# Moving the sums of the Strassen-like forms beside attention, and one rectified tile to VectorE

## The chip, the cores and the metric

The kernel runs on one core of a Trainium2 chip. The metric is device time in microseconds (us) of one execution. The times shown are three runs; a profiled execution gives the trace. Engines are named as the profile names them: PE (TensorE), PEld (its weight loads), DVE (VectorE), ACT (ScalarE), POOL (GpSimd), SP (SyncE, which issues nearly all DMAs).

## What is computed

Attention over 2 batches of 8 heads, 768 tokens and 64 columns a head, with a local window and global keys; its 1536 x 512 result x goes through a mixture of four experts, weighted by given probabilities, and then through a last layer.

```python
scores = scale * q @ k.T + bias          # bias: slope by head times distance; masked outside the window
a = exp(scores - max); a = a / (a.sum(-1) + 1e-09)
x = (a @ v) as (1536, 512)
for e in range(4):
    h = np.maximum(x @ w1[e], 0.0)       # 512 -> 1024
    out += p[:, e:e + 1] * (h @ w2[e])   # 1024 -> 512
h = out @ w_in; solu = h * softmax(h); ln = normalise(solu) * g_ln
result = ln @ w_out
```

All float32. Matmuls run on a pair of float32r parts: each operand is cast ("high") and the remainder ("low") is kept beside it, so each product is three matmuls (high by high, high by low, low by high).

## The kernel before

Each expert is cut into two half-experts, he = 0 to 7, of 512 hidden columns. The 1536 tokens are blocks of columns of the transposed x, held as `xh` and `xl`. For he = 0, `moe` (L644) goes over four blocks, (0, 256), (256, 256), (512, 512) and (1024, 512). In each block `gemm_groups` (L436) yields four groups `g1` (first product: 12 matmuls by `wR`, L452, then the rectified tile `fhh` on ACT, L458, and its remainder `fhl` on DVE, L459) and four groups `g2` (12 matmuls by `wV`, L471, then the scaling by the probabilities on DVE, L477 for he = 0 and L481 after, where POOL adds the result, L482). The first three blocks run inside attention; the fourth needs the last tokens and runs after it.

For he = 1 to 7 the third block goes as before, and the first 1024 tokens are taken as a pair: `paired_groups` (L498) forms two first products of 512 columns from seven smaller ones, with matrix forms of the Strassen kind. On the weights' side `form_steps` (L324, sums on POOL L337 to L340) makes the forms into `fwS` for each he. On x's side they are made once, by `x_forms` (L558): for j = 0 and 1 eight sums on POOL (`tt`, L575), four casts to high parts on ACT (`high`, L579) and four low parts on DVE (`low`, L582). Three forms go to `xt`; the fourth replaces `xh` and `xl` in columns 512 to 1023, which must no longer be needed raw.

`x_forms` is called when the fourth block of he = 0 begins (L659) and puts its steps into `st.due`; `tick` (L374), called after each group, carries out what is due, among the splits of the next weights (`split_of`: the high part on ACT, L288, the low part on POOL, L296), the weight forms and the loads. The steps of j = 0 and 1 stand five ticks apart, sixteen ticks in all: over the eight groups of he = 0's fourth block and the first seven of he = 1's third. `st.formed`, set by the last, lets the conversion of the last layer's weights start (`conv_steps`, L353, every third tick).

Attention is written out by hand in steps; from t = 14 each step takes two units of one token block and two heads (loop at L1156). In order: `scores` (L862, PE), `soft_pair` (L891), which normalises the probabilities `p` of the units t - 2 and t - 1 (DVE, L898 to L902), runs what is `late` (the low part `xl` of a finished token block, L975) and computes the masked scores (DVE, L915) and their exponentials (ACT, L920) of units t and t + 1; then `pull`, which lets `moe` issue groups up to a share of time; `stage_b` (transposes, L941, copied by ACT, L943); `pull` again; `stage_c` (the product with v, L963, and for a finished token block `xh` on ACT, L974). The last exponentials belong to t = 46; t = 48 and 50 finish. After the loop the last `late` makes the last `xl`, and `rest_of_moe` runs what is left. Every engine works its own queue in the order written here; the program fixes it.

Of the kernel before, what the change touches and what calls it, by code (L numbers as in the profile page):

```python
# [8 lines left out]
F32 = mybir.dt.float32  # L9
# [3 lines left out]
I64 = mybir.dt.int64  # L13
U32 = mybir.dt.uint32
AF = mybir.ActivationFunctionType
ALU = mybir.AluOpType
# [35 lines left out]
def kernel(ctx, tc, ep, qk, vp, nn, pr, wall, w64, gl, out):  # L52
# [158 lines left out]
    def stream(arm):  # L211
# [25 lines left out]
        st.rest = 0  # L237
        st.in_pb = 3 if arm == "f" else 0
        st.pre = None
        st.formed = False  # L240
        if arm == "f":

# [193 lines left out]
        def gemm_groups(he, blk, last, given=None):  # L436


            c0, n = blk
            cols = slice(c0, c0 + n)  # L440
            hh, hl = [None] * 4, [None] * 4

            def g1(ft):
                made = st.pre if he == 0 and c0 == 0 else None
                if made:
                    ps = made[ft]
                else:
                    ps = st.psp.tile([128, 512], F32, tag="g", name=f"{arm}g")
                w = st.pieces[8 * he + ft].rearrange("p w (k f) -> p w k f", k=4)
                for k in range(0 if made else 4):  # L450
                    for i, (a, b) in enumerate(((0, xh), (0, xl), (1, xh))):
                        nc.tensor.matmul(ps[:, :n], lhsT=w[:, a, k], rhs=b[:, k, cols],  # L452
                                         start=(k == 0 and i == 0), stop=(k == 3 and i == 2))
                    if k < 3:
                        yield 3 * n / 2.4
                th = st.hp.tile([128, n], F32R, tag="hh", name=f"{arm}hh")
                tl = st.hp.tile([128, n], F32R, tag="hl", name=f"{arm}hl")
                nc.scalar.activation(th, ps[:, :n], AF.Relu)  # L458
                nc.vector.scalar_tensor_tensor(out=tl, in0=ps[:, :n], scalar=0.0, in1=th.bitcast(F32),  # L459
                                               op0=ALU.max, op1=ALU.subtract)  # L460
                hh[ft], hl[ft] = th, tl
                if last and he == 0:
                    st.free["R", ft] = 1
                yield 3 * n / 2.4

            def g2(dt):
                ps = st.psp.tile([128, 512], F32, tag="g", name=f"{arm}g")
                w = st.pieces[8 * he + 4 + dt].rearrange("p w (k f) -> p w k f", k=4)
                for k in range(4):
                    for i, (a, b) in enumerate(((0, hh), (0, hl), (1, hh))):  # L470
                        nc.tensor.matmul(ps[:, :n], lhsT=w[:, a, k], rhs=b[k],  # L471
                                         start=(k == 0 and i == 0), stop=(k == 3 and i == 2))
                    if k < 3:
                        yield 3 * n / 2.4
                a = acc[:, dt, cols]
                if he == 0:
                    nc.vector.tensor_tensor(out=a, in0=ps[:, :n], in1=pb[:, cols], op=ALU.mult)  # L477
                else:
                    st.tk = getattr(st, "tk", 0) + 1
                    t = tmp2[:, st.tk % 2, :n]  # L480
                    nc.vector.tensor_tensor(out=t, in0=ps[:, :n], in1=pb[:, cols], op=ALU.mult)  # L481
                    nc.gpsimd.tensor_tensor(out=a, in0=a, in1=t, op=ALU.add)  # L482
                    if he == NHE - 1:
                        nc.scalar.copy(xh[:, dt, cols], a)
                        nc.gpsimd.tensor_tensor(out=xl[:, dt, cols], in0=a, in1=xh[:, dt, cols].bitcast(F32),
                                                op=ALU.subtract)
                if last:
                    st.free["V", dt] = he + 1
                    if he == NHE - 1 and dt < 2:
                        st.second.append(14 + dt)  # L490
                yield 3 * n / 2.4

            if given:
                hh, hl = given
                return [g2(i) for i in range(4)]
            return [g1(i) for i in range(4)] + [g2(i) for i in range(4)]
# [61 lines left out]
        def x_forms():  # L558

            g, v = nc.gpsimd, nc.vector  # L560
            hold = {}

            def temps(j):
                if j == 0:
                    hold[j] = [tmp2[:, 0], tmp2[:, 1], krf[:, 2048:2560]]
                else:
                    hold[j] = [st.cvp.tile([128, 256], I64, tag="r64", name=f"{arm}r64", bufs=2).bitcast(F32)
                               for _ in range(2)] + [krf[:, 2048:2560]]

            def steps(j):  # L570
                (b11, b12), (b21, b22) = ([[x[:, k, c0:c0 + HALF].bitcast(F32) for x in (xh, xl)] for c0 in (0, HALF)]
                                          for k in (j, 2 + j))

                def tt(out, in0, in1, op=ALU.subtract):
                    g.tensor_tensor(out=hold[j][out], in0=hold[j][in0] if isinstance(in0, int) else in0,  # L575
                                    in1=hold[j][in1] if isinstance(in1, int) else in1, op=op)

                def high(f, n):
                    nc.scalar.copy(f, hold[j][n])  # L579

                def low(f, h, n):
                    v.tensor_tensor(out=f, in0=hold[j][n], in1=h.bitcast(F32), op=ALU.subtract)  # L582

                def form(f):
                    return xt[:, f, 0, j], xt[:, f, 1, j]

                n4 = [x[:, j, HALF:2 * HALF] for x in (xh, xl)]

                def s0():
                    temps(j)  # L590
                    tt(0, b12[0], b12[1], ALU.add)
                    tt(1, b22[0], b22[1], ALU.add)

                def s1():
                    tt(2, 0, b11[0])
                    tt(2, 2, b11[1])

                def s2():
                    tt(0, 1, 0)

                def s3():
                    high(form(0)[0], 2)
                    tt(1, 1, 2)

                def s4():
                    high(form(2)[0], 0)
                    low(form(0)[1], form(0)[0], 2)

                def s5():
                    high(form(1)[0], 1)  # L610
                    low(form(2)[1], form(2)[0], 0)

                def s6():
                    low(form(1)[1], form(1)[0], 1)
                    tt(0, b21[0], 1)
                    tt(0, 0, b21[1], ALU.add)

                def s8():
                    high(n4[0], 0)

                def s9():
                    low(n4[1], n4[0], 0)
                    if j == 1:
                        st.formed = True

                return [s0, s1, s2, s3, s4, s5, s6, None, s8, s9]

            for j in range(2):
                for i, f in enumerate(steps(j)):
                    if f:  # L630
                        st.due.setdefault(st.now + 1 + 5 * j + i, []).append(f)

        st.x_forms = x_forms
        st.form_steps = form_steps
# [9 lines left out]
    def moe(st, first_blocks):  # L644
# [11 lines left out]
        for j, blk in enumerate(first_blocks):  # L656
            yield blk[0] + blk[1], 0.0
            if j == len(first_blocks) - 1:
                st.x_forms()  # L659
            yield from run(0, blk, j == len(first_blocks) - 1)  # L660
        for he in range(1, NHE):
            yield from run(he, (2 * HALF, 512), False)
# [130 lines left out]
    def fast_arm():  # L793
        st = stream("f")
        with ExitStack() as es:
# [15 lines left out]
            sps = psS.tile([128, 2, 2, 256], F32, name="sps")  # L811
            qs = {s: q_early[s] for s in range(3)}
            vts = {}
            st_p, st_rs, st_pt, st_x = {}, {}, {}, {}
            NU = 4 * NSLOT
            NAT = 2
            N0 = 4 * NAT
# [73 lines left out]
            def soft_pair(t):  # L891

                if t == PAIRS:
                    for _ in stage_n(t - 1):
                        pass
                elif t <= NU:
                    su = st_rs.pop(t - 2)
                    nc.vector.tensor_tensor(out=su, in0=su, in1=eps, op=ALU.add)  # L898
                    nc.vector.reciprocal(out=su, in_=su)
                    for u in (t - 2, t - 1):  # L900
                        p = st_p[u]
                        nc.vector.tensor_tensor(out=p, in0=p, in1=su[:, 2 * (u % 2):2 * (u % 2) + 2].unsqueeze(2)  # L902
                                                .to_broadcast([128, 2, 256]), op=ALU.mult)
                while late:
# [251 lines left out]
            for t in range(PAIRS, NU + 3, 2):  # L1156
# [18 lines left out]
                if t % 4 == 2:  # L1175
                    done = (t - 2) // 4
                    load_v(done + 1)
                if t < NU:
                    for u in (t, t + 1):
                        st.split_piece("act" if u < N0 + 12 and u % 2 else "dve", "pool")  # L1180
                        st.load_piece()
# [179 lines left out]
```

## Time and profile before

| what | value |
|---|---|
| median of 3 runs | 759.12 us (759.12 to 759.14) |
| the profiled execution | 758.87 us, span 757.1 us |
| mean granted clock of PE | 0.993 |
| PE busy | 736.8 us (97% of the span), 3710 matmuls |
| PEld busy | 598.6 us (79%) |
| DVE busy | 445.7 us (59%) |
| POOL busy | 305.1 us (40%) |
| ACT busy | 267.6 us (35%) |
| chain that ended last, by engine | PE 78%, issue 9%, POOL 8%, DVE 3%, ACT 2% |

The span is what the trace covers; the execution's own time has 1.8 us around it. Busy shares are averages over attention (to about 147 us), the half-experts (to about 617 us) and the last layer. PE's records overlap where it streams, so the time of a group is read from start to start.

### The profile page before, as it was taken

How to read it: one execution, taken by the hardware profiler on the slowest of the kernel's cores; microseconds unless marked ns; L12 is line 12 of the kernel's file. 1: busy time of each engine (PE TensorE's matmuls, PEld its weight loads, DVE VectorE, ACT ScalarE, POOL GpSimd, SP SyncE). 2: the span in 40 equal slices, each digit the busy share in tenths (PEclk: the TensorE clock that was granted, in tenths of full speed). 3: DMA queues.
4: the chain of work that ended last, by engine and by line, in shares of the span. 5: the costliest groups of instructions: out<-in, count | busy, mean ns of one | idle time of the engine just before them, and what ended most of it. 6: DMA issues, size and time to landing. Idle time of an engine off the chain costs nothing.

```text
span 757.1 us, 10591 instructions
## 1 busy us (share of the span) xinstructions
PE 736.8 (97%) x3710; PEld 598.6 (79%) x3710; DVE 445.7 (59%) x1026; ACT 267.6 (35%) x601; POOL 305.1 (40%) x294
## 2 busy tenths in 40 slices
PE   8889899998999999999999999999999999999997
PEld 6668777785788888888888888888887888888886
DVE  6777666434376667567577667767622427555541
ACT  5666675333232131231313214113132324233352
POOL 1000010089619708915942960981696271000001
PEclk9999999998999999999999999999999999999999
DMA  8544332011224323324422432441310630222221
GB/s 250 126 133 113 98 84 99 15 42 43 70 84 127 123 84 121 105 74 140 132 84 84 125 112 94 128 126 55 112 29 28 267 150 3 63 74 76 62 74 47
DMA packets 54014, 73.00 MB, mean 96 GB/s; under 512 B 7104, under 2 KB 31936, under 8 KB 53952
## 3 DMA queue, kind: packets, MB, share of 16 engines
q1 hardware_dynamic: 53392, 71.81, 31.3%
q8 instruction: 31, 0.51, 0.3%
q10 hardware_dynamic: 560, 0.43, 0.2%
q14 instruction: 31, 0.25, 0.1%
HBM read 56.46 MB, written 11.56 MB: 90 GB/s over the span
## 4 chain that ended last, share of the span: by engine, by line
PE 78%; issue 9%; POOL 8%; DVE 3%; ACT 2%; DMA 0%; POOLq 0%; ACTq 0%
PE fg L471 29%; PE fg L532 17%; PE fo L771 9%; PE fh L710 9%; PE fg L452 8%; PE sps L862 1%; PE pt L941 1%; POOL scr L482 1%; PE x L963 1%; POOL wV L296 1%; POOL fwS L296 1%; POOL fr L575 1%; POOL tmp L575 1%; ACT p L920 1%; PE wp L136 1%
## 5 line engine op out<-in xcount | busy, mean ns | idle before, releaser
L471 PE MATMUL fg<-fhh,wV 128*128 128x512 f32 (+1 forms) x800 | 248.4, 386 | 4.2 <-ACT fhh L458 3.1
L471 PEld LDWEIGHTS fg<-fhh,wV 128*128 128x128 f32 x800 | 149.9, 189 | 38.2 <-ACT fhh L458 4.4
L482 POOL TENSOR_TENSOR scr<-scr,tmp 128x512 f32<-128x512 f32 x84 | 108.3, 1293 | 165.2 <-DVE tmp L481 165.2
L471 PE MATMUL fg<-fhl,wV 128*128 128x512 f32 (+1 forms) x400 | 153.7, 384 | 1.2 <-DVE fhl L459 1.2
L481 DVE TENSOR_TENSOR tmp<-fg,pb 128x512 f32<-128x512 f32 x84 | 57.9, 689 | 74.5 <-PE fg L471 58.8
L452 PE MATMUL fg<-xh,wR 128*128 128x512 f32 (+1 forms) x320 | 99.5, 383 | 1.4 <-DVE xl L975 1.4
L471 PEld LDWEIGHTS fg<-fhl,wV 128*128 128x128 f32 x400 | 75.7, 189 | 16.7 <-DVE fhl L459 2.5
L452 PEld LDWEIGHTS fg<-xh,wR 128*128 128x128 f32 x320 | 59.5, 188 | 14.9 <-issue 2.0
L459 DVE SCALAR_TENSOR_TENSOR fhl<-fg,fhh 128x512 fp32r<-128x512 f32 (+1 forms) x40 | 26.6, 664 | 69.6 <-ACT fhh L458 69.2
L452 PE MATMUL fg<-xl,wR 128*128 128x512 f32 (+1 forms) x160 | 60.6, 379 | 0.0
L532 PE MATMUL fg<-xt,fwS 128*128 128x512 f32 x252 | 58.4, 390 | 1.0 <-ACT kr L537 1.0
L532 PEld LDWEIGHTS fg<-xt,fwS 128*128 128x128 f32 x252 | 47.2, 188 | 11.2 <-ACT kr L537 1.4
L537 ACT COPY kr<-fg 128x512 f32<-128x512 f32 x42 | 24.3, 584 | 89.4 <-PE fg L532 89.4
L296 POOL TENSOR_TENSOR wR<-fraw,wR 128x512 fp32r<-128x512 f32 x28 | 36.1, 1298 | 48.4 <-ACT wR L288 48.4
L532 PE MATMUL fg<-xh,wR 128*128 128x512 f32 x168 | 55.1, 394 | 0.0
L288 ACT CAST fwS<-kr 128x512 fp32r<-128x512 f32 x28 | 16.0, 619 | 95.0 <-POOL kr L340 95.0
L760 POOL TENSOR_SCALAR fva<-fva 128x1 f32<-128x1 f32 x12 | 3.8, 313 | 109.5 <-ACT scr L759 109.5
L920 ACT ACTIVATE p<-p,mn 128x256 f32<-128x256 f32 x68 | 33.8, 497 | 32.9 <-DVE mn L915 32.9
L771 PE MATMUL fo<-xt,fth 128*128 128x512 f32 (+1 forms) x156 | 45.3, 375 | 0.0
L458 ACT ACTIVATE fhh<-fg 128x512 fp32r<-128x512 f32 (+1 forms) x40 | 23.0, 574 | 54.5 <-PE fg L452 54.5
L519 ACT ACTIVATE fhh<-fg 128x512 fp32r<-128x512 f32 x42 | 24.2, 593 | 44.2 <-DVE fg L541 44.2
L520 DVE SCALAR_TENSOR_TENSOR fhl<-fg,fhh 128x512 fp32r<-128x512 f32 x42 | 28.3, 688 | 18.6 <-ACT fhh L519 18.6
(179 smaller groups left out, 1308.9 us busy)
## 6 DMA issues: line engine op xcount, KB each, us to landing
fraw<-in_wall_dram SPq DMA_DIRECT2D x61, 256.0 KB, 2.7
fr<-in_w_dram SPq DMA_DIRECT2D x32, 256.0 KB, 2.7
w_dram<-fr SPq DMA_DIRECT2D x32, 256.0 KB, 2.5
kr<-in_wall_dram SPq DMA_DIRECT2D x28, 256.0 KB, 2.7
v<-in_vp_dram SPq DMA_DIRECT2D x10, 512.0 KB, 3.6
xt<-w_dram SPq DMA_DIRECT2D x6, 512.0 KB, 10.0
kr<-in_qk_dram SPq DMA_DIRECT2D x22, 128.0 KB, 3.9
out_dram<-scr SPq DMA_DIRECT2D x11, 256.0 KB, 2.2
```

What stands on the lines that cost most here:

```text
L296: e.tensor_tensor(out=w[:, 1], in0=t, in1=w[:, 0].bitcast(F32), op=ALU.subtract)
L452: nc.tensor.matmul(ps[:, :n], lhsT=w[:, a, k], rhs=b[:, k, cols], start=(k == 0 and i == 0), stop=(k == 3 and i == 2))
L459: nc.vector.scalar_tensor_tensor(out=tl, in0=ps[:, :n], scalar=0.0, in1=th.bitcast(F32), op0=ALU.max, op1=ALU.subtract)
L471: nc.tensor.matmul(ps[:, :n], lhsT=w[:, a, k], rhs=b[k], start=(k == 0 and i == 0), stop=(k == 3 and i == 2))
L481: nc.vector.tensor_tensor(out=t, in0=ps[:, :n], in1=pb[:, cols], op=ALU.mult)
L482: nc.gpsimd.tensor_tensor(out=a, in0=a, in1=t, op=ALU.add)
L520: nc.vector.scalar_tensor_tensor(out=tl, in0=src, scalar=0.0, in1=th.bitcast(F32), op0=ALU.max, op1=ALU.subtract)
L532: nc.tensor.matmul(ps, lhsT=w[:, a, j], rhs=x[b][j], start=(i in (1, 2, 5) and j == 0 and m == 0), stop=(j == 1 and m == 2), skip_group_ch ...
L537: nc.scalar.copy(kept[q, i], ps)
L710: nc.tensor.matmul(ps[:, hf], lhsT=a[:, k, cs], rhs=w[:, b], start=(k == 0 and i == 0), stop=(k == 3 and i == 2))
L771: nc.tensor.matmul(ps, lhsT=a[:, fc % 4], rhs=wo[fc][:, b, c0:c0 + n], start=(fc == 0 and i == 0), stop=(fc == 7 and i == 2))
L920: nc.scalar.activation(p[:, a], p[:, a], AF.Exp, bias=mn[:, a:a + 1], scale=-1.0, accum_out=su[:, 2 * (u % 2) + a:2 * (u % 2) + a + 1])
```

## The change

**The sums.** `x_forms` returns eight lists of pieces of work and two last pieces, in place of due times. At attention's step t = 36 the lists are made; from then to t = 50 each step carries out one list at its end: two sums on POOL in each, and casts and low parts one to three steps behind their sums. Up to t = 48 a copy on POOL goes first, of one column of the step's second normalised tile into an unused cell, so that the step's sums start when its normalisations are done. The last two pieces (the fourth forms, which overwrite raw columns) and `st.formed` come where he = 0's fourth block begins. The temporary tiles are now parts of the accumulator that he = 0's fourth block writes later, and `tmp2`.

**The tile.** In he = 0's blocks that run in attention the fourth rectified tile is made on DVE, just ahead of its remainder, in place of ACT.

```diff
-                nc.scalar.activation(th, ps[:, :n], AF.Relu)
+                if ft == 3 and st.wS is None:
+                    nc.vector.tensor_scalar(th, ps[:, :n], 0.0, None, op0=ALU.max)
+                else:
+                    nc.scalar.activation(th, ps[:, :n], AF.Relu)
...
+            temps = [acc[:, j, 1024:1536] for j in range(4)] + [tmp2[:, j] for j in range(2)]
+            def of(j):
+                d12, d1, d2 = temps[3 * j:3 * j + 3]
...
+                add, less = ALU.add, ALU.subtract
+                return [lambda: sums((d12, b12[0], b12[1], add), (d1, d12, b11[0], less)),
+                        lambda: sums((d1, d1, b11[1], less), (d2, b22[0], b22[1], add)),
+                        lambda: sums((d12, d2, d12, less), (d2, d2, d1, less)),
+                        lambda: high(0, d1), lambda: high(2, d12), lambda: high(1, d2),
+                        lambda: low(0, d1), lambda: low(2, d12), lambda: low(1, d2),
+                        lambda: sums((d2, b21[0], d2, less), (d2, d2, b21[1], add)), last]
+            a, b = of(0), of(1)
+            st.unformed += [a[10], b[10]]
+            return [[a[0]], [a[1]], [a[2]], [a[3], b[0]], [a[4], a[6], b[1]], [a[5], a[7], b[2]],
+                    [a[8], b[3], b[4], b[5], a[9]], [b[6], b[7], b[8], b[9]]]
...
-                st.x_forms()
+                for step in (st.x_forms() if st.forms is None else st.forms):
+                    for f in step:
+                        f()
+                for f in st.unformed:
+                    f()
+                st.formed = True
...
                     for u in (t - 2, t - 1):
                         p = st_p[u]
+                        st_last[0] = p[:, 0, 0:1]
...
+                if t == 4 * 8 + 4:
+                    st.forms = st.x_forms()
+                if st.forms:
+                    if t <= NU:
+                        nc.gpsimd.tensor_copy(out=flg[:, 0:1], in_=st_last[0])
+                    for f in st.forms.pop(0):
+                        f()
```

Line numbers of the changed kernel differ a little; in the rows below L298 is L296 of before, L464 L459, L482 L477, L486 and L487 L481 and L482, L889 L915, L871 and L872 L898 and L899, L949 L975, L581 and L586 L582, and L1156 is the copy.

POOL from the end of the weight forms' sums to the scaled sums of he = 1's third block, before (`fr` and `tmp_72` hold the sums of x's forms):

```order
L575 TENSOR_TENSOR kr<-kr,xl 128x512
L296 TENSOR_TENSOR wV<-fraw,wV 128x512
L575 TENSOR_TENSOR fr_1959<-fr_1960,fr_1959 128x512
L296 TENSOR_TENSOR wV<-fraw,wV 128x512
L575 TENSOR_TENSOR fr_1960<-fr_1960,kr 128x512
L296 TENSOR_TENSOR fwS<-kr,fwS 128x512 x2
L296 TENSOR_TENSOR wV<-fraw,wV 128x512
L296 TENSOR_TENSOR fwS<-kr,fwS 128x512
L575 TENSOR_TENSOR fr_1959<-xh,fr_1960 128x512
L575 TENSOR_TENSOR fr_1959<-fr_1959,xl 128x512
L482 TENSOR_TENSOR scr<-scr,tmp_72 128x512
```

and with the change:

```order
L298 TENSOR_TENSOR wR<-fraw,wR 128x512
L298 TENSOR_TENSOR wV<-fraw,wV 128x512 x2
L298 TENSOR_TENSOR fwS<-kr,fwS 128x512 x2
L298 TENSOR_TENSOR wV<-fraw,wV 128x512
L298 TENSOR_TENSOR fwS<-kr,fwS 128x512
L487 TENSOR_TENSOR scr<-scr,tmp_72 128x512
L298 TENSOR_TENSOR wV<-fraw,wV 128x512
```

The sums of x's forms no longer stand between the low parts of the weights.

DVE in the last two steps of attention, before, from the last step's normalisations on:

```order
L902 TENSOR_TENSOR p<-p,su_1693 128x512 x2
L975 TENSOR_TENSOR xl<-x,xh 128x4x128
L477 TENSOR_TENSOR scr<-fg,pb 128x512 x2
L975 TENSOR_TENSOR xl<-x,xh 128x4x128
L459 SCALAR_TENSOR_TENSOR fhl<-fg,fhh 128x512 x4
```

and with the change:

```order
L949 TENSOR_TENSOR xl<-x,xh 128x4x128
L482 TENSOR_TENSOR scr<-fg,pb 128x512
L581 TENSOR_TENSOR xt<-scr,xt 128x512
L482 TENSOR_TENSOR scr<-fg,pb 128x512
L581 TENSOR_TENSOR xt<-tmp_72,xt 128x512
L581 TENSOR_TENSOR xt<-scr,xt 128x512
L581 TENSOR_TENSOR xt<-tmp_72,xt 128x512
L949 TENSOR_TENSOR xl<-x,xh 128x4x128
L586 TENSOR_TENSOR xl<-scr,xh 128x512
L586 TENSOR_TENSOR xl<-tmp_72,xh 128x512
L464 SCALAR_TENSOR_TENSOR fhl<-fg,fhh 128x512 x4
```

Three low parts now stand ahead of the last `xl`, and the two last ones behind it.

DVE at the fourth tile of the block (256, 256), with the change (before, the row L461 is not there, and ACT has one rectifier more):

```order
L889 ISA p,mn<-sps,btab 128x256
L889 ISA mn 128x1
L461 TENSOR_SCALAR fhh<-fg 128x256
L464 SCALAR_TENSOR_TENSOR fhl<-fg,fhh 128x256
L482 TENSOR_TENSOR scr<-fg,pb 128x256
L871 TENSOR_TENSOR su_1123<-su_1123,eps 128x4
L872 RECIPROCAL su_1123<-su_1123 128x4
```

The rectified tile now follows the step's masked scores directly, ahead of the next normalisation. PE's order is the same row by row.

## Rows read from the trace of the kernel before

**Rows 1.** The chain that ended last, in order of time: start us, us, what.

```profile
250.63 10.88 PE fg L471 x48
```

**Rows 2.** PE's timeline: start us, us, engine, line, operation, out<-in, count [idle before <-releaser].

```profile
179.78 0.39 PE L471 MATMUL fg<-fhh,wV 128*128 128x512 f32 x1
...
198.62 0.39 PE L532 MATMUL fg<-xh,wR 128*128 128x512 f32 x1
```

**Rows 3.** Busy time by stretches: PE, PEld, DVE, ACT, POOL; PE clock; DMA.

```profile
130.00:140.00 10.00, 10.00 (x74) 7.59 (x73) 7.21 (x22) 5.92 (x19) 0.00 (x0) 1.00 0.10 30
...
180.00:190.00 10.00, 7.09 (x17) 3.87 (x16) 8.10 (x8) 3.77 (x8) 10.00 (x8) 0.68 0.17 52
```

**Rows 4.** Waits of PE from 100 to 200 us: us in total, times, longest.

```profile
PE fg L471 <- ACT fhh L458: 1.5, 2, 1.0
...
PE fg L471 <- DVE fhl L459: 1.2, 1, 1.2
PE fg L471 <- POOL wV L296: 1.1, 2, 0.9
```

**Rows 5.** POOL's timeline in attention and just behind it.

```profile
103.00 2.54 POOL L575 TENSOR_TENSOR tmp<-xh,xl 128x512 f32<-128x512 f32 x2 [29.20 <-DVE xl L975]
153.97 1.29 POOL L296 TENSOR_TENSOR wR<-fraw,wR 128x512 fp32r<-128x512 f32 x1 [48.43 <-ACT wR L288]
```

**Rows 6.** PE's timeline in attention, at its waits and in two steps.

```profile
45.15 0.63 PE L941 MATMUL pt<-ident,p 128*128 128x128 f32 x4 [2.35 <-DVE p L931]
...
83.39 0.38 PE L471 MATMUL fg<-fhh,wV 128*128 128x256 f32 x1 [1.60 <-ACT fhh L458]
...
84.29 1.64 PE L963 MATMUL x<-pts,v 128*64 128x128 f32 x16
85.85 2.08 PE L862 MATMUL sps<-kr,q 64*128 64x256 f32 x8
...
90.81 1.09 PE L963 MATMUL x<-pts,v 128*64 128x128 f32 x16
91.84 1.13 PE L862 MATMUL sps<-kr,q 64*128 64x256 f32 x8
...
147.01 0.50 PE L452 MATMUL fg<-xh,wR 128*128 128x512 f32 x1 [1.41 <-DVE xl L975]
```

**Rows 7.** Timeline of DVE and POOL, single operations after attention.

```profile
161.55 0.68 DVE L582 TENSOR_TENSOR xt<-kr,xt 128x512 fp32r<-128x512 f32 x1
...
180.54 0.69 DVE L459 SCALAR_TENSOR_TENSOR fhl<-fg,fhh 128x512 fp32r<-128x512 f32 x1 [7.39 <-ACT fhh L458]
180.56 1.29 POOL L575 TENSOR_TENSOR fr<-fr,fr 128x512 f32<-128x512 f32 x1
...
182.32 1.75 DVE L582 TENSOR_TENSOR xt<-kr,xt 128x512 fp32r<-128x512 f32 x1
```

**Rows 8.** Costliest groups: a one-column operation of POOL.

```profile
L760 POOL TENSOR_SCALAR fva<-fva 128x1 f32<-128x1 f32 x12 | 3.8, 313 | 109.5 <-ACT scr L759 109.5
```

**Rows 9.** DVE's timeline in attention, at the fourth tile, beside sums, at the end.

```profile
81.85 0.08 DVE L915 DVE_READ_ACCUMULATOR2_ANT mn<- 128x1 f32 x1
83.37 0.42 DVE L459 SCALAR_TENSOR_TENSOR fhl<-fg,fhh 128x256 fp32r<-128x256 f32 x1 [1.44 <-ACT fhh L458]
...
103.17 0.42 DVE L915 CUSTOM_DVE_ANT_0 p<-sps,btab 128x256 f32<-128x256 f32 x1
...
144.61 0.69 DVE L477 TENSOR_TENSOR scr<-fg,pb 128x512 f32<-128x512 f32 x1 [4.20 <-PE fg L471]
146.26 0.69 DVE L975 TENSOR_TENSOR xl<-x,xh 128x512 fp32r<-128x512 f32 x1 [0.96 <-ACT xh L974]
```

**Rows 10.** ACT's timeline, the last copies of transposed probabilities.

```profile
140.92 1.07 ACT L943 COPY pts<-pt 128x512 f32<-128x512 f32 x2 [2.19 <-PE pt L941]
```

**Rows 11.** Busy time by stretches, at two waits of attention.

```profile
42.00:46.00 4.00, 1.66 (x14) 1.31 (x13) 3.14 (x13) 1.71 (x6) 0.00 (x0) 1.00 0.28 74
...
86.00:88.00 2.00, 2.00 (x9) 1.18 (x9) 0.45 (x2) 0.00 (x0) 0.00 (x0) 0.50 0.00 0
```

More of the change, by code (lines that the diff above doesn't have):

```diff
@@ L239, in stream @@
         st.pre = None
+        st.unformed = []
+        st.forms = None
         st.formed = False
@@ L560, in x_forms @@
             g, v = nc.gpsimd, nc.vector
[L561 to L570, printed above, removed]
+            temps = [acc[:, j, 1024:1536] for j in range(4)] + [tmp2[:, j] for j in range(2)]
@@ L571, in steps @@
+            def of(j):
+                d12, d1, d2 = temps[3 * j:3 * j + 3]
                 (b11, b12), (b21, b22) = ([[x[:, k, c0:c0 + HALF].bitcast(F32) for x in (xh, xl)] for c0 in (0, HALF)]
                                           for k in (j, 2 + j))
-                def tt(out, in0, in1, op=ALU.subtract):
-                    g.tensor_tensor(out=hold[j][out], in0=hold[j][in0] if isinstance(in0, int) else in0,
-                                    in1=hold[j][in1] if isinstance(in1, int) else in1, op=op)
@@ L578, in high @@
[L578 to L631, printed above, removed]
+                def sums(*ops):
+                    for out, in0, in1, op in ops:
+                        g.tensor_tensor(out=out, in0=in0, in1=in1, op=op)
@@ new lines, in high, with low, last @@
+                def high(f, t):
+                    nc.scalar.copy(xt[:, f, 0, j], t)
+                def low(f, t):
+                    v.tensor_tensor(out=xt[:, f, 1, j], in0=t, in1=xt[:, f, 0, j].bitcast(F32), op=ALU.subtract)
+                def last():
+                    h, l = xh[:, j, HALF:2 * HALF], xl[:, j, HALF:2 * HALF]
+                    nc.scalar.copy(h, d2)
+                    v.tensor_tensor(out=l, in0=d2, in1=h.bitcast(F32), op=ALU.subtract)
+                add, less = ALU.add, ALU.subtract
@@ L813, in fast_arm @@
             vts = {}
-            st_p, st_rs, st_pt, st_x = {}, {}, {}, {}
+            st_p, st_rs, st_pt, st_x, st_last = {}, {}, {}, {}, {}
             NU = 4 * NSLOT
```

## The prediction

> **What bounds the kernel now.** I read the clock first (it is granted in full nearly everywhere), then the chain that ended last, the busy time by stretches, the waits of TensorE, and at each wait the timelines of the engines around it. The chain is mostly matmuls: a group of 48 takes 10.88 us [rows 1], so from the end of attention on TensorE is the bound and only its waits can be won. They lie in three places. The first product group of half-expert 1 that multiplies by wV runs from 179.78 to 198.62, 18.84 us for 48 matmuls [rows 2]: 18.84 - 10.88 = 7.96 us lost. In 180 to 190 GpSimd is busy for all of the 10.00 us and TensorE's granted clock averages 0.68 [rows 3]. TensorE's waits there are for the tiles of ScalarE and VectorE (1.5 and 1.2 us) and for GpSimd's wV (1.1 us) [rows 4]; the rest of the 7.96 us is mostly matmuls at the lower clock. Behind all of them stands one queue: GpSimd, idle for 48.43 us up to 153.97 [rows 5], then has the forms' sums, the weights' differences and the weight forms' sums at once, ScalarE's casts wait for those sums, and its rectifiers stand behind the casts. The second place is 83.39 in attention: TensorE had waited 1.60 us for ScalarE's rectified fourth tile [rows 6]. The third is the end of attention, 1.41 us before 147.01 [rows 6].
>
> **The sums of the forms.** Sixteen sums leave the stretch around the first pass: two stood at 103.00 (2.54 us for both), fourteen after 153.97 [rows 5]. At 1.27 us each the fourteen are 17.8 us of GpSimd's time, and with them go six of the eight casts and six of the eight subtractions on the other engines; the last two of each come ahead of the block's first tiles, where TensorE has four products (10.88 us) before it needs any. What is left for GpSimd up to the product group is 4 differences for wR, 8 half-size sums, 4 for wV and 4 for wS. At 1.29 us (a full-size operation) [rows 7] for every one that is at most 20 x 1.29 = 25.8 us, in a stretch of 36 us (153.97 to wV's last use near 190). wV's last two pieces are cast behind the last rectifier; with what then stands ahead on GpSimd (one wV piece, one wS, one scaled sum) the last is ready two short ScalarE operations and four of GpSimd after the first wV tile is due, about 1.0 + 4 x 1.29 = 6.2 us, and is itself due 8.2 us (three tiles of 10.88 / 4) after it. So I take the whole **7.96 us** as won. The later half-experts have this same queue and no waits of TensorE in the views, which is why I do not shave it. Bounds: all of it, or the 1.1 us on wV kept with one stretch at the lower clock, about 2.5 us kept.
>
> In attention the sums meet idle engines. In 130 to 140 GpSimd does nothing, ScalarE is busy 5.92 and VectorE 7.21 us of 10, TensorE all 10.00 [rows 3], so about 2.8 us of VectorE is free in each 10 us. Each step gets two sums and at most one cast and one subtraction until the last two steps. The copy of the probabilities holds the sums until both normalisations of the step are done; behind it on GpSimd wait only the sums, and their casts come one or two steps later. The copy of one column is not in the trace; GpSimd's nearest operation on one column takes 0.31 us [rows 8], so copy and two sums stay under 3 us of a step of some 6 us (score products at 85.85 and 91.84) [rows 6], and end before the next normalisation. The next step's masked scores overwrite the tile that is copied; they come after that normalisation too. I cost the fourteen gated sums, six casts and first three subtractions at nothing: the cover is that idle time, and TensorE's matmuls; if it were gone, each subtraction would cost 0.68 us. The collision that matters is between GpSimd and a VectorE operation with two inputs in SBUF: the subtraction takes 0.68 us at 161.55 and 1.75 us at 182.32, when GpSimd has the turn, while one with an input in PSUM keeps 0.69 us at 180.54 beside a running sum [rows 7]. The masked scores, which also read PSUM, keep 0.42 us at 103.17, inside the two sums of 103.00 [rows 5, 9]. The normalisations have both inputs in SBUF, so the gate is what keeps them out of this.
>
> **The last subtractions.** In the last step three subtractions stand on VectorE between the last product's scaling (144.61) and the last xl (146.26) [rows 9]. Their casts on ScalarE follow the two copies of 140.92 (1.07 us) [rows 10]; three more of that size end near 143.6, in time. VectorE is free at 145.22; three times 0.61 us (0.68 less overlap) gives 147.05 in place of 146.26: **0.8 us** lost, since TensorE waits for that xl. If GpSimd were running beside them it would be 3 x 1.75, or 4.2 us; but its last two sums wait for the third subtraction, so I take 0.8 and keep 4.2 as the end. The last two sums (2.5 us) then end near 149.6 and hold a cast and a rectifier at about 150, ahead of which TensorE has work until 158.
>
> **The fourth tile.** Three rectifiers move to VectorE. In the blocks of columns 0 and 512, TensorE did not wait for them, and VectorE had stood idle for ScalarE; nothing won, 0.4 to 0.7 us more work on VectorE. In the block of columns 256 VectorE ended its masked scores at 81.93 and idled 1.44 us until ScalarE, behind four exponentials, had the tile [rows 9]. The operation is not in the trace: its nearest row is VectorE's own subtraction on this shape, 0.42 us; the ends are nothing and the 0.69 us of 512 columns at 144.61. I take 0.42, the same shape: the rectified tile at 82.3, its remainder at 82.7, where the remainder ended at 83.79 (83.37 + 0.42). Won: **1.1 us** (0.8 to 1.5); of the wait, which began at 81.79, about 0.5 us stays, and 0.25 us for the remainder. After that wait the clock fell: 86 to 88 shows 0.50 [rows 11], the 1.2 GHz level; from 84.29 to the end of the score products the records run 1.64 and 2.08 us where 1.09 and 1.13 are usual [rows 6]: 0.55 + 0.95 = **1.5 us**, won too if the wait that is left no longer lowers the clock. VectorE can follow, since it then waited for the score products.
>
> How likely is that? The gap of 2.35 us before 45.15 did not lower the clock (42 to 46 shows 1.00) [rows 6, 11], that of 1.41 us did not, that of 1.60 us did. So I take the clock as kept at 83, where the gap is shortest of these, and as kept in the new 2.2 us gap at the end of attention. The Trainium skill, "TensorE: Matmul & The Clock Gate", section HAM oscillation — how this bites in real kernels, ties the fall to long idle gaps alone, longer than any here. By that rule the wait of 1.60 us is not what lowered the clock, and the 1.5 us might stay; the sum would be -8.3 instead of -9.8. The trace contradicts the rule's strict form, since the clock did fall there.
>
> **The rest.** The conversion of the last layer's weights starts one conversion earlier, loads and stores with it; each lands in the same place of a later pass and TensorE does not wait on it. SyncE's queue keeps the weight loads in order. Matmuls are unchanged in number and order.
>
> **Sum.** -7.96 + 0.8 - 1.1 - 1.5 = **-9.8 us**. The profiled execution took 758.87 us (span 757.1 and 1.8 around it): 749.1. The median of the runs is 0.25 above it: **749.3 us**. A difference under 0.2%, 1.5 us, could not be told from no change.
>
> **The rivals.**
> - One fall of the clock more than I assume: it stays low after 83 (1.5 us not won) or falls in the 2.2 us gap (a stretch like that of 84 to 88, about 1.6 us). For: the fall after 1.60 us. Against: 2.35 us without one. 750.8 us; chance 0.25. By the rule above the first would hold.
> - The queue still blocks in half-expert 1: wV's last pieces wait for their casts, behind the rectifiers. 2.5 us kept: 751.8 us; chance 0.10. Against: the later half-experts.
> - The change does not do what it says at the fourth tile: TensorE waits next for the exponentials' consumer, VectorE, just as long, and nothing of 2.6 us comes. 751.9 us; chance 0.06.
> - Slower: VectorE becomes the bound of attention. If the gate lets sums fall upon the two normalisations of each of seven steps and on six subtractions, at 1.75 - 0.68 = 1.07 us each, that is 20 x 1.07 = 21.4 us; VectorE's 2.8 us per 10 us over 45 us hide 12.6; 8.8 are left, and a wait of over a microsecond in every step would hold the clock low, 0.95 us each, 6.7 us. -9.8 + 15.5 = +5.7: 764.8 us. It decides from 1.4 us a step on. Against: GpSimd's time per step and the gate. Chance 0.05.
> - Gains eaten to the last 1.5 us by a milder form of it: 759; chance 0.03.
>
> My forecast keeps 0.51. Its own range is 747.3 to 750.0 (downward: transposes in attention that wait some tenths for VectorE now). To hold 8 in 10 the range takes in the first three rivals: **747.2 to 752.8**. Faster 0.92, same 0.03, slower 0.05.
>
> **What would show it.** Right: GpSimd busy in 103 to 150 with sums in pairs behind a small copy, at 1.27 us, no operation of VectorE over 0.7 us; the first wV group of half-expert 1 at 10.9 us and clock 1.00; TensorE's wait at 83 at half a microsecond; the last wait of attention near 2.2 us. Wrong: subtractions or normalisations at 1.1 us and more in attention, transposes waiting for them, a wV wait left, or a clock of 0.5 after either gap.

## The result, and the profile after

The changed kernel takes **748.53 us** (median of 4 runs, 748.18 to 749.49), the kernel before in the same session 759.12 (757.99 to 759.14). The ratio is 0.9866, with an interval of 0.9849 to 0.9883: faster by 10.6 us. The profiled execution took 748.74 us, its span 746.9, 10.2 us less than before.

In the changed kernel L476 is the former L471 (product by wV), L454 the former L452 (by wR), L537 the former L532, L915 the transposes, L949 the low part xl, L876 the normalisation, L461 and L463 the rectifiers on DVE and ACT.

The chain that ended last, in order of time (start us, us, what), from the end of attention on:

```profile
144.50 11.15 PE fg L454 x48
...
177.41 10.88 PE fg L476 x48
188.29 19.21 PE fg L537 x84
...
240.15 10.88 PE fg L476 x48
```

The first wV group of half-expert 1 starts at 177.41 and takes 10.88 us, where it took 18.84 [rows 2]. The group that began at 250.63 [rows 1] begins at 240.15, 10.48 us earlier. The spans differ by 10.2 us: 0.3 us is given back behind the last product, where the span ends 5.2 us after it in place of 4.9.

PE's waits, whole span (us in total, times, longest):

```profile
PE pt L915 <- DVE p L905: 3.5, 3, 2.3
PE fg L454 <- DVE xl L949: 2.2, 1, 2.2
...
PE fg L476 <- DVE fhh L461: 0.5, 1, 0.5
```

The waits for wV, the rectified tiles and their remainders [rows 4] are gone; the wait at the fourth tile is 0.5 us, the last one of attention 2.2.

Busy time by stretches (PE, PEld, DVE, ACT, POOL; PE clock; DMA), to be read against [rows 3, 11]:

```profile
46.00:48.00 2.00, 2.00 (x22) 1.65 (x23) 1.55 (x8) 2.00 (x10) 0.00 (x0) 1.00 0.00 0
86.00:88.00 2.00, 2.00 (x20) 1.86 (x21) 0.97 (x6) 2.00 (x10) 0.00 (x0) 1.00 0.00 0
130.00:140.00 10.00, 10.00 (x71) 8.01 (x73) 6.33 (x17) 6.48 (x17) 4.59 (x5) 1.00 0.07 26
180.00:190.00 10.00, 10.00 (x46) 8.29 (x45) 5.21 (x11) 0.23 (x1) 8.29 (x7) 1.00 0.24 79
```

POOL, idle between 130 and 140 before, now works 4.59 us there; from 180 to 190 it has 1.7 us to spare and the clock is 1.00. POOL's timeline in two steps, and at the end of attention:

```profile
104.27 0.19 POOL L1156 COPY flg<-p 128x1 f32<-128x1 f32 x1 [1.69 <-DVE p L876]
104.41 1.30 POOL L575 TENSOR_TENSOR scr<-scr,xl 128x512 f32<-128x512 f32 x1
105.67 1.28 POOL L575 TENSOR_TENSOR scr<-xh,xl 128x512 f32<-128x512 f32 x1
111.83 0.18 POOL L1156 COPY flg<-p 128x1 f32<-128x1 f32 x1 [4.88 <-DVE p L876]
...
143.93 1.27 POOL L575 TENSOR_TENSOR tmp<-xh,tmp 128x512 f32<-128x512 f32 x1 [3.44 <-DVE xt L581]
145.28 1.62 POOL L575 TENSOR_TENSOR tmp<-tmp,xl 128x512 f32<-128x512 f32 x1
```

The copy waits for the normalisation (L876), costs 0.18 to 0.19 us, and the pair of sums stands behind it. PE's timeline at its wait for the fourth tile and at its last wait in attention (idle before in brackets), and ahead of them two groups of transposes in the block of columns 0:

```profile
49.33 1.03 PE L915 MATMUL pt<-ident,p 128*128 128x128 f32 x8
53.91 1.06 PE L915 MATMUL pt<-ident,p 128*128 128x128 f32 x8
...
81.91 0.39 PE L476 MATMUL fg<-fhh,wV 128*128 128x256 f32 x1 [0.53 <-DVE fhh L461]
...
144.50 0.50 PE L454 MATMUL fg<-xh,wR 128*128 128x512 f32 x1 [2.16 <-DVE xl L949]
```

Before, the same two groups of transposes stood at 49.39 and 54.24 and took 1.23 us each:

```profile
49.39 1.23 PE L941 MATMUL pt<-ident,p 128*128 128x128 f32 x8
54.24 1.23 PE L941 MATMUL pt<-ident,p 128*128 128x128 f32 x8
```

### The profile page after: what moved, and what is told of

The parts are those of the page before. It is cut to its first block, busy times and chain, and to the rows that moved or that the text cites. A ratio compares the mean times of both kernels' runs of the same rounds, so it can differ in the third digit from the quotient of the medians.

```text
span 746.9 us, 10608 instructions
## 1 busy us (share of the span) xinstructions
PE 730.4 (98%) x3710; PEld 596.6 (80%) x3710; DVE 443.7 (59%) x1029; ACT 266.3 (36%) x598; POOL 304.5 (41%) x301
## 4 chain that ended last, share of the span: by engine, by line
PE 85%; POOL 5%; DVE 4%; ACT 2%; issue 2%; DMA 0%; POOLq 0%; ACTq 0%
PE fg L476 31%; PE fg L537 16%; PE fg L454 12%; PE fo L744 9%; PE fh L683 9%; PE x L937 2%; PE sps L835 2%; PE pt L915 2%; POOL scr L487 2%; PE wp L136 1%; PE wp L1010 1%; POOL fwS L298 1%; DVE p L876 1%; POOL xl L490 1%; ACT p L894 0%
## 5 line engine op out<-in xcount | busy, mean ns | idle before, releaser
L476 PE MATMUL fg<-fhh,wV 128*128 128x512 f32 (+1 forms) x800 | 246.0, 383 | 0.5 <-DVE fhh L461 0.5
L487 POOL TENSOR_TENSOR scr<-scr,tmp 128x512 f32<-128x512 f32 x84 | 108.4, 1295 | 167.2 <-DVE tmp L486 167.2
L476 PEld LDWEIGHTS fg<-fhh,wV 128*128 128x128 f32 x800 | 148.9, 188 | 32.3 <-issue 3.0
L476 PE MATMUL fg<-fhl,wV 128*128 128x512 f32 (+1 forms) x400 | 152.3, 381 | 0.1
L486 DVE TENSOR_TENSOR tmp<-fg,pb 128x512 f32<-128x512 f32 x84 | 57.9, 689 | 76.6 <-PE fg L476 65.7
L454 PE MATMUL fg<-xh,wR 128*128 128x512 f32 (+1 forms) x320 | 99.5, 383 | 2.2 <-DVE xl L949 2.2
L476 PEld LDWEIGHTS fg<-fhl,wV 128*128 128x128 f32 x400 | 75.1, 188 | 14.4 <-DVE fhl L464 0.3
L454 PEld LDWEIGHTS fg<-xh,wR 128*128 128x128 f32 x320 | 59.5, 188 | 15.7 <-DVE xl L949 2.4
L464 DVE SCALAR_TENSOR_TENSOR fhl<-fg,fhh 128x512 fp32r<-128x512 f32 (+1 forms) x40 | 26.6, 665 | 59.6 <-ACT fhh L463 59.3
L454 PE MATMUL fg<-xl,wR 128*128 128x512 f32 (+1 forms) x160 | 60.6, 378 | 0.0
L537 PE MATMUL fg<-xt,fwS 128*128 128x512 f32 x252 | 58.4, 390 | 1.0 <-ACT kr L542 1.0
L537 PEld LDWEIGHTS fg<-xt,fwS 128*128 128x128 f32 x252 | 47.2, 188 | 11.2 <-ACT kr L542 1.4
L537 PE MATMUL fg<-xh,wR 128*128 128x512 f32 x168 | 55.1, 394 | 0.0
L463 ACT ACTIVATE fhh<-fg 128x512 fp32r<-128x512 f32 (+1 forms) x38 | 22.0, 580 | 60.3 <-PE fg L454 60.3
L298 POOL TENSOR_TENSOR wV<-fraw,wV 128x512 fp32r<-128x512 f32 x28 | 36.1, 1299 | 13.4 <-ACT wV L290 13.4
```

Of the source, the lines that this page charges most:

```text
L298: e.tensor_tensor(out=w[:, 1], in0=t, in1=w[:, 0].bitcast(F32), op=ALU.subtract)
L476: nc.tensor.matmul(ps[:, :n], lhsT=w[:, a, k], rhs=b[k], start=(k == 0 and i == 0), stop=(k == 3 and i == 2))
L537: nc.tensor.matmul(ps, lhsT=w[:, a, j], rhs=x[b][j], start=(i in (1, 2, 5) and j == 0 and m == 0), stop=(j == 1 and m == 2), skip_group_ch ...
```

## The experiments

The theory: GpSimd's queue in half-expert 1 costs 7.96 us, the fourth tile some 2.6 us with the clock, and the gate keeps sums off the normalisations. Rivals: the gain comes mostly from one of the two edits; the gate does nothing; the clock would have fallen anyway. The runs were made in two sets, each on one chip and each with the kernel before beside them: 758.17 us (median of 11) in the first set, 759.03 (of 9) in the second. Ratios are to the kernel before in the same set. The first set has the first four experiments, the second the others.

**The sums alone**, the change with the fourth tile back on ACT:

```
-                if ft == 3 and st.wS is None:
+                if ft == 4:
```

> The sums stand beside attention as in the change; the fourth rectified tile goes back to ScalarE in all three blocks. Theory (the terms are separate): 7.96 us from the product group of half-expert 1, less 0.75 us at the end of attention, and nothing else: 759.1 - 7.2 = 751.9 us (751.4 to 752.4). TensorE waits 1.6 us for the fourth tile near 83 again, and the clock shows 0.50 in 86 to 88. Rival (the sums' move itself took away the fall of the clock or some of the wait in attention): 748.5 to 750 us, and no stretch at 0.50.

Measured 751.81 us (750.54 to 753.2), ratio 0.9914 [0.99, 0.9929]. PE's timeline and the clock (same columns as above) in its profiled execution:

```profile
45.19 0.63 PE L915 MATMUL pt<-ident,p 128*128 128x128 f32 x4 [2.34 <-DVE p L905]
...
83.93 0.38 PE L476 MATMUL fg<-fhh,wV 128*128 128x256 f32 x1 [1.59 <-ACT fhh L463]
```

```profile
46.00:48.00 2.00, 2.00 (x14) 1.77 (x14) 0.56 (x5) 2.00 (x9) 0.00 (x0) 0.50 0.00 0
86.00:88.00 2.00, 2.00 (x17) 1.62 (x18) 1.94 (x7) 0.45 (x2) 0.00 (x0) 1.00 0.00 0
```

The wait for the tile is back in full, but the clock did not fall behind it: in this execution it fell behind the gap of 2.34 us at 45, and stayed at 1.00 from 84 to 88. The wV group took 10.88 us (179.62 to 190.50).

**The tile alone**, the kernel before with the fourth tile on DVE:

```
+                if ft == 3 and st.wS is None:
+                    nc.vector.tensor_scalar(th, ps[:, :n], 0.0, None, op0=ALU.max)
+                else:
+                    nc.scalar.activation(th, ps[:, :n], AF.Relu)
```

> The kernel before with the fourth tile on VectorE and the sums where they were. Theory: the wait near 83 falls from 1.6 to 0.5 us (1.1), the stretch at the lower clock goes (1.5) and the earlier blocks give 0.5: 759.1 - 3.1 = 756.0 us (755.5 to 756.6), with the first wV group of half-expert 1 still at 18 to 19 us. Rival (attention's gain is swallowed, since GpSimd's queue after it sets the time and does not start earlier): 758 to 759 us, with a longer wV group.

Measured 755.82 us (755.34 to 756.79), ratio 0.9963 [0.9948, 0.9977]. PE's waits still hold half-expert 1's stalls, the clock averages 0.66 in 180 to 190, and the wV group takes 18.83 us (176.59 to 195.42):

```profile
PE fg L474 <- ACT fhh L461: 1.5, 2, 1.0
...
PE fg L474 <- DVE fhl L462: 1.2, 1, 1.2
PE fg L474 <- POOL wV L296: 1.1, 2, 0.9
```

In the traces the two edits are separate. The sums alone leave the wait at the fourth tile as it was and take the stall out of the wV group. The tile alone ends attention 3.20 us earlier (143.81 for 147.01) and keeps the stall. In the medians they win 6.4 and 2.4 us, 8.7 together, where the change won 10.6 beside its first result and 9.2 in the second set; the medians show no more than that they add up within some 2 us.

**The tile of one block.** The edit kept in the block of columns 256 alone:

```
-                if ft == 3 and st.wS is None:
+                if ft == 3 and c0 == 256 and st.wS is None:
```

> The change with the fourth tile on VectorE only in the block of columns 256; the blocks of columns 0 and 512 go back to ScalarE. Theory: the block of columns 0 gave 0.5 us, because VectorE's next normalisation came earlier and the transposes of the next two steps (49.3 and 53.9) no longer waited; without it they take 1.23 us again and the time is 749.0 us (748.8 to 749.4). Rival (as the prediction had it, those two blocks are worth nothing): 748.5 us, transposes at 1.03 us.

Measured 749.6 us (749.33 to 750.3), ratio 0.9883 [0.9865, 0.9901], a little above the expected range. The change itself is not in this set; the next version, which has all three tiles, took 748.5, but 0.7 us of that difference is its own edit's. In the trace the score products in the block of columns 0 stand at 47.82, 52.76 and 57.59, steps of 4.94 and 4.83 us, where the change has 47.45, 52.02 and 56.64, steps of 4.57 and 4.62. The transposes of these steps take 1.23 us again:

```profile
49.85 1.23 PE L915 MATMUL pt<-ident,p 128*128 128x128 f32 x8
54.70 1.23 PE L915 MATMUL pt<-ident,p 128*128 128x128 f32 x8
```

So the tile of that block does win, 0.58 us over two steps. The medians alone would not settle a difference of that size.

**The last three low parts behind xl.** The last step's list goes behind the last `late`:

```
-                if st.forms:
-                    if t <= NU:
-                        nc.gpsimd.tensor_copy(out=flg[:, 0:1], in_=st_last[0])
+                if st.forms and t <= NU:
+                    nc.gpsimd.tensor_copy(out=flg[:, 0:1], in_=st_last[0])
...
+            for f in st.forms.pop(0):
+                f()
```

> The change with the last step's list (three subtractions and two sums) put behind the last xl. Theory: the three subtractions ahead of that xl cost 0.75 us; the last wait of attention falls from 2.2 to 1.4 us and the time to 747.8 us (747.4 to 748.2). Rival (the wait is set by ScalarE's xh or by the banks, so the subtractions filled time that was idle anyway): 748.5 us and a wait near 2.2 us.

Measured 748.5 us (747.79 to 749.14), ratio 0.9868 [0.985, 0.9887]. The median is the one that the rival named, not the theory's 747.8, but the rival's wait of 2.2 us is not there: PE's last wait in attention is 1.41 us again.

```profile
143.78 0.50 PE L454 MATMUL fg<-xh,wR 128*128 128x512 f32 x1 [1.41 <-DVE xl L949]
```

The product starts at 143.78 instead of 144.50, so 0.72 us is won in the trace; the medians, of runs spread over a microsecond, can't show it.

**The change again**, for comparison within the second set.

> The change as it is, beside the runs of this call, so that they can be compared on one chip. Theory: 748.0 to 749.5 us, ratio 0.987, with executions in two groups about 1.2 us apart by whether the clock fell in one of the two gaps (near 83 or near 143). Rival (the spread has another source): no relation between an execution's time and its mean granted clock.

Measured 749.79 us (748.54 to 750.23), ratio 0.9875 [0.986, 0.989]. Its profiled execution is instructive, since the clock fell in it, though at neither place that was expected (83 and 143). PE's timeline, and stretches:

```profile
45.22 0.78 PE L915 MATMUL pt<-ident,p 128*128 128x128 f32 x4 [2.34 <-DVE p L905]
```

```profile
46.00:48.00 2.00, 2.00 (x12) 1.78 (x12) 1.56 (x8) 2.00 (x10) 0.00 (x0) 0.50 0.00 0
86.00:88.00 2.00, 2.00 (x18) 2.00 (x19) 1.43 (x8) 1.51 (x7) 0.00 (x0) 1.00 0.00 0
146.00:148.00 2.00, 2.00 (x10) 1.64 (x9) 0.71 (x1) 0.10 (x1) 1.78 (x2) 1.00 0.03 8
```

The next score products start at 48.90, against 47.45 in the other profile of the same program: 1.45 us lost behind the same gap of 2.34 us. By 129.81, against 128.85, 0.96 us of it is left, since a later TensorE waits less for VectorE.

The two groups that were expected are there. Of the eight runs of the change, four beside its first result and four here, the four with a mean granted clock of 0.998 took 748.18 to 748.74 us and the four with 0.996 took 749.36 to 750.23. One execution of each group was profiled: the one without a fall in attention is in the first, this one in the second. For the other six the mean clock is a sign and no proof, since it also takes in the span's end behind the last product, where the clock stands at 0.50 as well (744 to 746 in the change).

**No gate.** The copy is left out, so that the sums start as soon as their inputs are there:

```
-                    if t <= NU:
-                        nc.gpsimd.tensor_copy(out=flg[:, 0:1], in_=st_last[0])
```

> The change without the copy of the normalised probabilities, so the sums run as soon as their inputs stand. Theory (the gate keeps the sums off the normalisations): twelve sums run in a row from about 100 to 116, two or three steps' normalisations take over 1 us in place of 0.69, transposes wait for them, and the time is 0.3 to 1.0 us above the change's. Rival (the gate is worth nothing, since the step has room): the same time within 0.2 us, although some operations are longer.

Measured 753.83 us (751.62 to 754.26), ratio 0.9932 [0.9918, 0.9946]: 4.0 us slower than the change in the same set, four times the upper end of what was expected. POOL's, DVE's and PE's timelines, and DVE's line L876 (14 operations; shortest, median and longest in ns):

```profile
102.90 1.27 POOL L575 TENSOR_TENSOR scr<-scr,xl 128x512 f32<-128x512 f32 x1
104.13 1.75 POOL L575 TENSOR_TENSOR scr<-xh,xl 128x512 f32<-128x512 f32 x1
105.96 2.98 POOL L575 TENSOR_TENSOR scr<-scr 128x512 f32<-128x512 f32 x2
```

```profile
103.09 3.34 DVE L876 TENSOR_TENSOR p<-p,su 128x512 f32<-128x512 f32 x2
...
111.91 3.21 DVE L876 TENSOR_TENSOR p<-p,su 128x512 f32<-128x512 f32 x2
```

```profile
L876 DVE TENSOR_TENSOR p<-p,su x14: 684/692/1786, 93.4 to 131.7; 128x512 f32<-128x512 f32 x14
```

```profile
113.59 0.63 PE L915 MATMUL pt<-ident,p 128*128 128x128 f32 x4 [0.65 <-DVE p L876]
115.27 0.63 PE L915 MATMUL pt<-ident,p 128*128 128x128 f32 x4 [1.04 <-DVE p L876]
```

Twelve sums run back to back from 100.15 on. Two pairs of normalisations fall among them and take 3.34 and 3.21 us, where a pair takes 1.29 with the gate: (3.34 - 1.29) / 2 = 1.02 us more for each of the first pair and 0.96 for each of the second. TensorE waits 0.65 and 1.04 us for them, and leaves attention at 147.49 instead of 144.50. Of these 2.99 us, 0.24 stood before the first sum (score products at 97.81 for 97.57), so the collision cost some 2.7. This execution, 751.62, is the quickest of the five and held the clock (0.999); the others took 753.7 to 754.3 at mean clocks of 0.993 to 0.995. That their further 2 us are falls of the clock is likely, but none of them was profiled.

**The sums on VectorE.** The kernel before, with the sixteen sums on DVE at their old due times:

```
-                    g.tensor_tensor(out=hold[j][out], in0=hold[j][in0] if isinstance(in0, int) else in0,
+                    v.tensor_tensor(out=hold[j][out], in0=hold[j][in0] if isinstance(in0, int) else in0,
```

> The kernel before with the sixteen sums on VectorE in place of GpSimd, at their old due times; casts and low parts as they were, the fourth tile on ScalarE. Theory (GpSimd's queue holds up half-expert 1): the sums take 0.6 to 0.7 us each on VectorE, GpSimd's queue is as free as in the change, and the first wV group falls from 18.8 to 11 to 13 us: 5.5 to 8 us under the kernel before. Rival (the casts ahead of the rectifiers on ScalarE, or VectorE's own work, hold it up): less than 3 us under it, wV group above 16 us.

Measured 750.27 us (750.22 to 750.35), ratio 0.9883 [0.9868, 0.9899]: 8.8 us won with the sums where they were, by taking them out of GpSimd's queue. They did not get shorter, though 0.6 to 0.7 us each was expected: on VectorE they took 0.68 to 1.79 us, twelve of the sixteen over 1.17, where GpSimd had taken 1.27 to 1.78. POOL's first operation after attention, PE's first products of the wV group and of the group behind it, and the stretch that held the stall:

```profile
152.81 1.28 POOL L296 TENSOR_TENSOR wR<-fraw,wR 128x512 fp32r<-128x512 f32 x1 [77.77 <-ACT wR L288]
```

```profile
178.62 0.39 PE L471 MATMUL fg<-fhh,wV 128*128 128x512 f32 x1
...
190.04 0.39 PE L532 MATMUL fg<-xh,wR 128*128 128x512 f32 x1
```

```profile
180.00:190.00 10.00, 9.88 (x43) 7.71 (x42) 7.71 (x9) 1.06 (x2) 8.04 (x6) 1.00 0.20 62
```

The wV group runs from 178.62 to 190.04, 11.42 us: 7.42 of the 7.96 us are back. In its profiled execution, too, the clock fell behind the gap at 45 and not behind the wait of 1.59 us at 83.86. So 1.1 us of the 8.7 between the profiled spans is not the sums' but that of another place of the fall: attention ends at 145.87 in place of 147.01.

**All four tiles on VectorE**, with the last low parts behind xl: the edit of the last three low parts above, and

```
-                if ft == 3 and st.wS is None:
+                if st.wS is None:
```

> All four rectified tiles of the three blocks in attention on VectorE, and the last low parts behind the last xl. Theory: VectorE no longer waits 1.44 us for ScalarE at the second and third tile of the block of columns 256, where its loop holds up the transposes; the step of the score products near 62 to 77 falls from 4.9 to 5.5 to about 4.85 us, 0.9 us, and 0.7 us come from the low parts: 1.6 us under the change, 746.9 us. Rival (3.9 us more work make VectorE the bound of attention): at or above the change's time, with transposes that wait for normalisations.

Measured **745.66 us** (745.43 to 746.83), ratio 0.9826 [0.9812, 0.9839]: 4.1 us under the change in the same set, more than the 1.6 that were expected, and the fastest version of the study. Three of the four runs of the change in this set are of the group at 0.996, so about 1 us of the 4.1 is likely the clock's. DVE's waits from 60 to 90 us, in the change and in this version:

```profile
DVE fhl L464 <- ACT fhh L463: 5.3, 3, 2.4
DVE scr L482 <- PE fg L476: 1.6, 2, 1.0
DVE su L871 <- ACT p L894: 0.5, 1, 0.5
```

```profile
DVE scr L482 <- PE fg L476: 1.6, 2, 1.0
DVE su L871 <- ACT p L894: 1.3, 3, 0.5
DVE fhh L461 <- PE fg L454: 0.5, 1, 0.5
```

With the first three tiles on ACT, DVE stood for 5.3 us at their remainders, with the normalisations behind them in its queue. Those waits are gone, and so are PE's of 0.20, 0.26 and 0.53 us for DVE (74.24, 79.09 and 81.91 in the change): score products start at 71.43, 76.36, 81.48 and 86.42 in place of 71.64, 77.14, 83.83 and 88.77, 2.35 us earlier at the last. Most of it, 1.57 us, lies in the step that holds the fourth tile, where the expectation had looked for 0.9 us in the steps before. The end of attention adds 0.75, which makes 3.1 us between the profiled spans (743.8 and 746.9). Four of its five runs lie within 0.4 us, at a mean clock of 1.00.

## Why the prediction was right, and where it was off

Forecast 749.3 us, measured 748.53, inside the range and with the sign right. By its steps, between the two profiled executions:

- **The sums: -7.96 forecast, -7.96 measured** (18.84 to 10.88 us). That the cause was GpSimd's queue, and not the stretch as such, the sums on VectorE show: 7.42 of it came back with the sums where they were, and no shorter.
- **The last subtractions: +0.8 forecast, +0.75 measured** (2.16 less 1.41 us of wait). Moving the last three low parts behind xl takes it away again. The last pair of sums ends at 146.9, not at 149.6, and holds nothing up.
- **The wait for the fourth tile: -1.1 forecast, -1.07 measured** (1.60 to 0.53 us).
- **The clock behind that wait: -1.5 forecast, -1.6 between these two executions**, but the step that gave it failed (which gaps lower the clock). The score products of 85.85 and 91.84 [rows 6] stand at 83.83 and 88.77: 3.07 us earlier at the second, of which 0.4 came before and 1.07 is the wait. The prediction ordered the gaps by what lowers the clock, "that of 2.35 us did not, that of 1.60 us did", and took the rest of the wait as too short. In three profiled executions (the sums alone, the change again, the sums on VectorE) the clock fell behind the gap of 2.34 us, and in two of these the wait of 1.59 us came later and no fall behind it. In the before profile it was the other way round. The length of a gap thus does not order them. Whether it falls behind either gap differs from execution to execution. With the tile on VectorE one of its two places is gone: one of three profiled executions with the wait of 1.6 us fell there, none of seven with 0.53 us or no wait. What that is worth on average is not shown; the tile alone won 2.4 us in the medians (1.7 to 3.9 by the interval), of which the wait and the first block make some 1.6; that leaves about 0.8 for the clock, an estimate, in place of 1.5. The other half of the step, that the 2.2 us gap at the end of attention keeps the clock, held in all five executions that have it. By the Trainium skill, "TensorE: Matmul & The Clock Gate", section HAM oscillation — how this bites in real kernels, gaps of this length would not lower the clock; the traces disagree, at 0.50 behind 1.60 us and behind 2.34 us. The first rival, one fall more, is what the change's second profile shows, but behind the gap at 45, which the prediction took as safe, and at a net 0.96 us in place of 1.5.
- **"Nothing won" in the blocks of columns 0 and 512** failed for the first: 0.60 us over two steps (score products at 47.35 and 57.14 before, 47.45 and 56.64 after). For the block of columns 512 it held: the products of 118.67 before come 3.09 us earlier, against 3.07 at 91.84. In the block of columns 0 TensorE did not wait for the tile, as the prediction said; but its transposes began up to 0.16 us later after the score products and stretched to 1.23 us, behind a VectorE that had idled for ScalarE's tile. With the tile on VectorE they take 1.03 and 1.06, and the kernel with the tile in one block alone loses 0.58 us. The prediction named such tenths for the transposes only as a lower edge of its range.
- **The cover of the fourteen sums held.** No subtraction of attention lies over 0.73 us and no pair of normalisations over 1.30, and the copies cost 0.19 us, under the 0.31 of [rows 8]. The sign "no operation of VectorE over 0.7 us" missed: behind the last xl a subtraction of the fourth form takes 1.38 us from 144.37 on, beside the ungated sum of 143.93; nothing waited for it. The slower rival's mechanism is real without the gate, and its price, 1.07 us for a normalisation, measured 1.02 and 0.96; it struck four of the fourteen, so it cost 2.7 us in the trace and 4.0 in the medians, not the 15.5 that this rival named.

The trace before held a sign against ordering the gaps by their length: at half-expert 1's stall the clock fell near 184, behind a wait of 1.03 us and within the next, of 1.17, both shorter than the gap of 1.41 us that kept it.

```profile
184.73 0.80 PE L471 MATMUL fg<-fhl,wV 128*128 128x512 f32 x1 [1.17 <-DVE fhl L459]
```

```profile
184.00:186.00 2.00, 1.22 (x2) 0.50 (x2) 1.75 (x3) 0.77 (x2) 2.00 (x2) 0.50 0.37 131
```

The sum of the five terms as measured, -7.96 + 0.75 - 1.07 - 1.6 - 0.4 (what is left of the first block's 0.60 when the fourth tile comes), is -10.3; the profiled span fell by 10.2. Forecast and profiled execution lie 0.4 us apart (749.1 and 748.74), which is the term left out. The other 0.4 us by which the median beat the forecast is spread, and luck: the forecast put the median 0.25 above the profiled execution and it came 0.21 below, with three of the four runs in the group without the fall. In the second set three of four are in the other group, and the same program has a median of 749.79, on the other side of the forecast and still inside both ranges.

## What to carry to other kernels

A stall late in a kernel can be a queue that an idle engine could have worked off earlier: look for where that engine was idle, and price the move by what it slows there: here a normalisation beside a sum took about 1 us more. Where two engines collide, one tiny operation that reads the other's last result puts them in turn, for 0.2 us a time of the engine that has room. An engine that idles at one operation is late with everything behind it in its queue, so price an edit that ends such a wait also where TensorE doesn't wait for that operation itself.

## What the runs showed of the hardware that was not expected

The same program, with the same gap of 2.34 us before 45.2, ran on at full clock in one profiled execution and at 0.50 from 46 to 48 in another; the fall cost 1.45 us there and 0.96 by the end of attention. Of ten profiled executions four had one fall in attention, and none had two: three behind this gap, which nine of the ten have at 2.34 or 2.35 us, and one behind the wait of 1.60 us. A microsecond of the spread between runs of one program thus needs no other cause, though what decides which execution is struck stays open.
